# One fused attention and feed-forward block: a 2048-wide in-place VectorE exp chain, K fills by DMA, packs in one DMA, and an immediate exp bias

## The chip, the cores and the metric

The kernel runs on one core of a Trainium2 chip (trn2). The metric is the device time of one execution in microseconds (us). The median of three runs of the kernel before was 967.28 us (966.4 to 967.91). "Granted clock" is the TensorE clock that the throttle allowed, as a share of full speed.

Engine names in the profile: PE is the TensorE matmul, PEld its weight load, DVE is VectorE, ACT is ScalarE, POOL is GpSimd, SP is SyncE, which issues the DMAs.

## The reference

```python
# x [1, 2048, 512], 32 heads of 16, F = 1792, all bf16
xn = layernorm(x)
q, k, v = split(xn @ wqkv)                      # [1, 32, 2048, 16] each
p = softmax(q @ k.T * 16 ** -0.5)               # 32 x 2048 x 2048 scores
attn = (p @ v) reshaped @ wo
ffn = (silu(xn @ w1) * (xn @ w3)) @ w2          # "gate", "up", "down"
return x + attn + ffn
```

The 134 million exponentials of the softmax are the bulk of the elementwise work. In tiles of 128 x 1024 they are 1,024 tiles.

## The kernel before

The program is put in order when it is built: a small scheduler keeps a clock for each engine, with assumed durations (`dur=`), and places each instruction where it believes the engine to be free.

**Exponentials on two engines.** TensorE makes a 128 x 1024 tile of scores in PSUM. ScalarE turns most tiles into probabilities with one instruction; it has two PSUM buffers for this. VectorE takes the others through a chain of five instructions on the bits of a bf16 number (the scores come out of the matmul already scaled, so that their integer value is a bit pattern): `p1` reads PSUM, `m`, `e`, `g` split and shape the bits, `t` multiplies (in this order). The sum of `e`, `g` and `t`, made by three matmuls with V, is an approximate exponential.

```python
# ScalarE
P.op("act", lambda e: e.activation(PT[:, s_, :], ps[:, b0 * 512:(b0 + 2) * 512], ACTF.Exp,
                                   scale=ASC, bias=act_bias[:, 0:1]), ...)       # L1550
# VectorE, per tile of 1024
e.tensor_scalar(yb, ps[:, 4*512:6*512], 0.0, 32767.0, ALU.max, ALU.min)          # L1593 p1
e.tensor_scalar(dsl[.., 0], yb, 0x7F80, None, ALU.bitwise_and)                   # L1610 e
e.tensor_scalar(mb, yb, 0x7F, 0x3F00, ALU.bitwise_and, ALU.bitwise_or)           # L1616 m
e.tensor_scalar(dsl[.., 1], yb, -352.0, 0.0, ALU.add, ALU.max)                   # L1621 g
e.tensor_tensor(dsl[.., 2], yb, mb, ALU.mult)                                    # L1627 t
# ...
```

**K fills and packs.** Heads of 16 are padded to 32 partitions. The padding rows of K and Q must hold a constant, written once per group of heads (the "fills"), two groups on ScalarE and six on GpSimd. Then the real rows are moved from a staging tile by DMA (the "packs"), four DMAs of 16 partitions for each half:

```python
for g in range(2, NG):                                                           # L1157
    ... P.op("pool", lambda e: e.tensor_scalar(KT[:, g, :], sel1[:, 0:1].to_broadcast((128, S)), YB, None, ALU.mult), ...)

for j in range(4):                                                               # L1283
    m = P.dma(lambda e, j=j: e.dma_start(dst(hh)[32 * j:32 * j + 16, :],
                                         stg[64 * hh + 16 * j:64 * hh + 16 * j + 16, sl, :]), ...)
```

Of the kernel before, what the change touches and what calls it, by code (L numbers as in the profile page):

```python
# [137 lines left out]
_LAT = 0.09  # L138
# [839 lines left out]
def _plan_fast(nc, ps, flag, A_x, A_wqkv, A_wo, B_w1, B_w3, B_w2, out):  # L978
# [18 lines left out]
    ND = 3  # L997
# [4 lines left out]
    D_LAST = RPU - 6  # L1002
    NW = 3

# [6 lines left out]
    with ctx:  # L1011
        xd = sb("xd", [128, max(NT * D, ND * 3 * 1024)], I16)
        x_sb = xd[:, 0:NT * D].bitcast(BF16).rearrange("p (t d) -> p t d", d=D)
        dsl = xd[:, 0:ND * 3 * 1024].rearrange("p (s k n) -> p s k n", k=3, n=1024)
        xr = sb("xr", [128, 2, D], BF16)
        yb = sb("yb", [128, 2, 1024], I16)
        mb = sb("mb", [128, 2, 1024], I16)
# [4 lines left out]
        lnb = sb("lnb", [128, NT], FP32)  # L1022
        lnt = sb("lnt", [128, NT], FP32)
        act_bias = sb("act_bias", [128, 1], FP32)
# [8 lines left out]
        stg = sb("stg", [128, 3, 512], BF16)  # L1033
        sel = sb("sel", [128, 4], FP32)
        sel1 = sb("sel1", [128, 1], FP32)
        onorm = sb("onorm", [128, NON, 512], BF16)
# [35 lines left out]
        a_cost = lambda n: 0.113 + 0.000835 * n  # L1072
        d_cost = lambda n: 0.095 + 0.00104 * n


        def c_misc(e):
            e.memset(ones_t[:, :], 1.0)
            e.memset(mhalf[:, :], -0.5)
            e.memset(act_bias[:, :], -127.0 * math.log(2.0) + math.log(KAPPA))
            return e.memset(Vaug[:, :, :, 16:17], 1.0)  # L1080
# [5 lines left out]
        for gi in range(1, 4):  # L1086
            P.dma(lambda e, gi=gi: e.dma_start(x_sb[:, 4 * gi:4 * gi + 4, :], x_v[:, 4 * gi:4 * gi + 4, :]),
                  writes=[("x", t) for t in range(4 * gi, 4 * gi + 4)], kb=512)
            if gi == 1:
                P.dma(lambda e: e.dma_start(wv, wqkv_v[:, :, 2 * D:3 * D]), writes=[("wv",)], kb=512)  # L1090

        P.op("dve", lambda e: e.memset(bank(7), 0.0), writes=[("ps", 7)], dur=0.6)
        P.op("pool", lambda e: e.memset(sel[:, :], 1.0), writes=[("sel",)], dur=0.1)
        P.op("pool", lambda e: e.affine_select(sel[:, :], sel[:, :], [[-32, 4]], ALU.is_equal, 0.0,
                                               base=-16, channel_multiplier=1),
# [3 lines left out]
        P.op("act", lambda e: e.activation(QT[:, :, :].rearrange("p a n -> p (a n)"),  # L1099
                                           sel1[:, 0:1].to_broadcast((128, 4 * 512)), ACTF.Identity),  # L1100
             reads=[("sel1",)], writes=[("QT", i) for i in range(4)], dur=1.9)
        for g in range(2):
            P.op("act", lambda e, g=g: e.activation(KT[:, g, :], sel1[:, 0:1].to_broadcast((128, S)), ACTF.Identity,
                                                    scale=YB),
                 reads=[("sel1",)], writes=[("KT", g, i) for i in range(NQC)], dur=1.9)
        P.op("pool", c_misc, writes=[("ones_t",), ("mhalf",), ("abias",)] + [("V", t) for t in range(NT)], dur=0.8)
# [4 lines left out]
        def ln_coef(gi, n0, n1):  # L1111
            sl_ = slice(n0, n1)
            MVK = [("mv", t) for t in range(n0, n1)]

            def f(eng):
                P.op("pool", lambda e: e.tensor_scalar(lnt[:, sl_], mv[:, sl_, 1], 1.0, EPS, ALU.mult, ALU.add),
                     reads=MVK + [("mhalf",)], writes=[("lnt", n0)], dur=0.12)
                P.op("pool", lambda e: e.tensor_tensor(lnr[:, sl_], lnt[:, sl_], mhalf[:, sl_], ALU.pow),
                     reads=[("lnt", n0)], writes=[("lnr", n0)], dur=0.7)
                P.op("pool", lambda e: e.tensor_tensor(lnt[:, sl_], mv[:, sl_, 0], lnr[:, sl_], ALU.mult),  # L1120
                     reads=[("lnr", n0)] + MVK, writes=[("lnt", n0)], dur=0.12)
                o = P.op("pool", lambda e: e.tensor_scalar(lnb[:, sl_], lnt[:, sl_], -1.0, 0.0, ALU.mult, ALU.add),  # L1122
                         reads=[("lnt", n0)], writes=[("lnb", n0)], dur=0.12)
                for t in range(n0, n1):
                    P.post("dve", lambda t=t: norm(t), ready=o.end + _LAT, prio=1)
            return f
# [4 lines left out]
        def norm(t):  # L1131
            n0 = nrm0[t]
            xs = t % 4
            o = P.op("dve", lambda e: e.tensor_scalar(xn_sb[:, xs, :], x_sb[:, t, :], lnr[:, t:t + 1], lnb[:, t:t + 1],  # L1134
                                                      ALU.mult, ALU.add),
                     reads=[("x", t), ("lnr", n0), ("lnb", n0)], writes=[("xn", xs)], dur=0.25)
# [20 lines left out]
        for g in range(2, NG):  # L1157
            P.post("pool", lambda g=g: done.__setitem__(("KTi", g), P.op("pool", lambda e: e.tensor_scalar(
                KT[:, g, :], sel1[:, 0:1].to_broadcast((128, S)), YB, None, ALU.mult),
                reads=[("sel1",)], writes=[("KT", g, i) for i in range(NQC)], dur=2.5).end), ready=9.0 + g, prio=3)  # L1160
# [103 lines left out]
        def pack(dst, keys, dkeys, scale):  # L1264

            def evac(bk, o, rel):
                sl = stg_n[0] % 3
# [13 lines left out]
                def moves(hh):  # L1281
                    for j in range(4):
                        m = P.dma(lambda e, j=j: e.dma_start(dst(hh)[32 * j:32 * j + 16, :],  # L1283
                                                             stg[64 * hh + 16 * j:64 * hh + 16 * j + 16, sl, :]),
                                  reads=[("stg", sl), ("sel1",)] + keys[hh], writes=[dkeys[hh] + (j,)], kb=16)
                    done[dkeys[hh]] = m.end + _LAT
# [3 lines left out]
        def tile_KT(i, sc):  # L1290
            xc = xdone(sc * 512, 512)
            gr = []
            for c in range(DC):
# [4 lines left out]
                lambda hh: KT[:, 2 * i + hh, sc * 512:(sc + 1) * 512],  # L1298
# [3 lines left out]
        def tile_QT(qc, i):  # L1302
# [3 lines left out]
            for c in range(DC):  # L1306
# [4 lines left out]
                lambda hh: QT[:, (u0 + hh) % 4, :],  # L1311
# [122 lines left out]
        st = {"pos": 0, "pv": 0, "dpar": 0, "nd": 0, "lastA": -1.0, "n_exp": 0, "dpos": 0}  # L1434
# [3 lines left out]
        ds_free = [0.0] * ND  # L1438
# [57 lines left out]
        def score(b0, name, dur):  # L1496
# [6 lines left out]
            rd = [("QT", u % 4), ("KT", g, kt // 4)]  # L1503
            mms = []
            for i in range(2):
                j = j0 + i
                rd += [("QTm", u, j), ("KTm", g, kt // 4, j)]
# [7 lines left out]
            o = P.op("pe", f, reads=rd, writes=[("ps", b0), ("ps", b0 + 1)], dur=dur, name="%s%d" % (name, r0))  # L1515
# [7 lines left out]
        def try_a():  # L1523
# [11 lines left out]
            x = score(2 * buf, "A", 0.27)  # L1535
# [10 lines left out]
            def emit():  # L1546
# [4 lines left out]
                                                       scale=ASC, bias=act_bias[:, 0:1]),  # L1551
                         reads=[("ps", b0), ("ps", b0 + 1), ("abias",)], writes=[("PT", s_)], dur=a_cost(1024))
# [11 lines left out]

        def try_d():
# [3 lines left out]
            if r0 % RPU > D_LAST or r0 < st["dpos"]:  # L1569
                return False  # L1570
            if r0 % 4 != st["dpar"]:
                return False
            x = score(4, "D", 0.09 if st["lastA"] + 0.05 > P.t else 0.27)
# [8 lines left out]
            nd = st["nd"]  # L1582
            st["nd"] += 1
            ys = nd % 2

            def slot():
                return [s_ for s_ in range(ND) if ds_free[s_] <= P.t]

            def p1():
                s_ = slot()[0]  # L1590
                ds_free[s_] = 1e9
                left = [6]
                q = P.op("dve", lambda e: e.tensor_scalar(yb[:, ys, :], ps[:, 4 * 512:6 * 512], 0.0, 32767.0,  # L1593
                                                          ALU.max, ALU.min),
                         reads=[("ps", 4), ("ps", 5)], writes=[("yb", ys)], dur=1.24)
                dbuf[0] = q.end + _LAT

                def rel(o_):
                    left[0] -= 1
                    if left[0] == 0:  # L1600
                        ds_free[s_] = o_.end + _LAT

                def give(k, q_):
                    st["n_exp"] += (k == 2) * 2
                    for i in range(2):
                        add_task(u, j0 + i, kt, dsl[:, s_, k, 512 * i:512 * i + 512].bitcast(BF16), q_.end + _LAT,
                                 ("ds", s_, k), rel)

                def f_e():
                    q_ = P.op("dve", lambda e: e.tensor_scalar(dsl[:, s_, 0, :], yb[:, ys, :], 0x7F80, None,  # L1610
                                                               ALU.bitwise_and),
                              reads=[("yb", ys)], writes=[("ds", s_, 0)] + XD, dur=0.34)
                    give(0, q_)

                def f_m():
                    P.op("dve", lambda e: e.tensor_scalar(mb[:, ys, :], yb[:, ys, :], 0x7F, 0x3F00,  # L1616
                                                          ALU.bitwise_and, ALU.bitwise_or),
                         reads=[("yb", ys)], writes=[("mb", ys)], dur=0.34)

                def f_g():  # L1620
                    q_ = P.op("dve", lambda e: e.tensor_scalar(dsl[:, s_, 1, :], yb[:, ys, :], -352.0, 0.0,  # L1621
                                                               ALU.add, ALU.max),
                              reads=[("yb", ys)], writes=[("ds", s_, 1)] + XD, dur=0.34)
                    give(1, q_)

                def f_t():
                    q_ = P.op("dve", lambda e: e.tensor_tensor(dsl[:, s_, 2, :].bitcast(BF16),  # L1627
                                                               yb[:, ys, :].bitcast(BF16), mb[:, ys, :].bitcast(BF16),
                                                               ALU.mult),
# [289 lines left out]
```

## Time and profile before

| | before |
|---|---|
| median of the runs | 967.28 us |
| span of the profiled run | 968.4 us |
| ScalarE busy | 853.9 us, 88% |
| VectorE busy | 878.7 us, 91% |
| exponential tiles, ScalarE / VectorE | 798 / 226 |
| ScalarE idle, 0 to 80 us | 46.5 us |
| ScalarE idle, 80 to 926.5 us | 28.0 us |
| after the last exponential | 41.9 us |

These are the busy row of the page and the main groups. A group's columns are: line, engine, operation, what it writes and reads, count, then busy us in all and mean ns of one, then the engine's idle time just before the group and what ended most of it.

```profile
PE 858.6 (89%) x9033; PEld 240.4 (25%) x9033; DVE 878.7 (91%) x1437; ACT 853.9 (88%) x872; POOL 91.4 (9%) x82
...
L1550 ACT ACTIVATE f_PT<-ps,f_act_bias 128x1024 bf16<-128x1024 f32 x798 | 819.1, 1153 | 51.3 <-PE ps L1513 44.1
...
L1593 DVE TENSOR_SCALAR f_yb<-ps 128x1024 int16<-128x1024 f32 x226 | 274.4, 1214 | 5.3 <-PE ps L1513 4.9
...
L1346 ACT ACTIVATE f_th<-ps 128x512 f32<-128x512 f32 x56 | 35.2, 629 | 10.6 <-PE ps L1216 10.6
...
L1134 DVE TENSOR_SCALAR f_xn_sb<-f_xd,f_lnr,f_lnb 128x512 bf16<-128x512 bf16 x16 | 35.3, 2244 | 0.3 <-POOL f_lnb L1122 0.3
```

Read the first group twice. Its mean is 1153 ns, but 819.1 us divided by 798 is 1.026 us: consecutive exponentials overlap in the records, and the busy time counts overlapped time once. The 1.026 is what one more exponential costs a busy ScalarE.

The table by stretches of time gives each engine's busy time in each (PEclk is the granted clock):

```profile
core 0: us, PE busy (x) PEld busy (x) DVE busy (x) ACT busy (x) POOL busy (x), PEclk, DMA share, GB/s
...
20.00:40.00 20.00, 10.87 (x112) 4.12 (x104) 20.00 (x24) 5.50 (x9) 16.08 (x13) 0.70 0.44 80
...
80.00:300.00 220.00, 192.55 (x1844) 50.12 (x1844) 197.99 (x327) 199.93 (x203) 9.33 (x7) 0.94 0.23 30
300.00:600.00 300.00, 283.55 (x3009) 76.60 (x3006) 288.33 (x485) 296.20 (x301) 16.37 (x12) 0.99 0.25 29
600.00:926.50 326.50, 304.69 (x3188) 82.92 (x3186) 312.74 (x522) 322.40 (x331) 15.93 (x12) 0.99 0.25 33
926.50:968.40 41.90, 28.92 (x469) 12.55 (x469) 12.50 (x24) 1.82 (x4) 0.00 (x0) 0.86 0.20 36
```

From 80 to 926.5 us ScalarE works 818.5 of 846.5 us. From 20 to 40 us it works 5.5 of 20 us while VectorE is busy all the time. The timeline shows with what (start, duration):

```profile
25.58 0.72 DVE L1134 TENSOR_SCALAR f_xn_sb<-f_xd,f_lnr,f_lnb 128x512 bf16<-128x512 bf16 x2
26.82 10.83 DVE L1134 TENSOR_SCALAR f_xn_sb<-f_xd,f_lnr,f_lnb 128x512 bf16<-128x512 bf16 x2
...
26.77 10.73 POOL L1158 TENSOR_SCALAR f_KT<-f_sel 128x2048 bf16<-128x2048 f32 x2
```

A pair of normalising instructions takes 0.72 us alone, and the next such pair 10.83 us while GpSimd fills K. The Trainium skill, "SBUF — State Buffer", SBUF: two separate sides, describes a port pair which VectorE and GpSimd share as an exclusive lock, held for the whole instruction; this trace agrees with it.

### The profile page before, as it was taken

How to read it: one execution, taken by the hardware profiler on the slowest of the kernel's cores; microseconds unless marked ns; L12 is line 12 of the kernel's file. 1: busy time of each engine (PE TensorE's matmuls, PEld its weight loads, DVE VectorE, ACT ScalarE, POOL GpSimd, SP SyncE). 2: the span in 40 equal slices, each digit the busy share in tenths (PEclk: the TensorE clock that was granted, in tenths of full speed). 3: DMA queues.
4: the chain of work that ended last, by engine and by line, in shares of the span. 5: the costliest groups of instructions: out<-in, count | busy, mean ns of one | idle time of the engine just before them, and what ended most of it. 6: DMA issues, size and time to landing. Idle time of an engine off the chain costs nothing.

```text
span 968.4 us, 21733 instructions
## 1 busy us (share of the span) xinstructions
PE 858.6 (89%) x9033; PEld 240.4 (25%) x9033; DVE 878.7 (91%) x1437; ACT 853.9 (88%) x872; POOL 91.4 (9%) x82
## 2 busy tenths in 40 slices
PE   4669888989888999998989999999999999999985
PEld 2222122222222222222222222222222222222232
DVE  7969797999899999999999999999999999999951
ACT  3339798999899999999999999999999999999930
POOL 7840000000000000000000000000000000000000
PEclk9779799999989999999999999999999999999988
DMA  4501221312311222303232222222231212233221
GB/s 154 136 16 28 37 39 23 50 22 27 51 13 13 24 19 24 46 17 41 29 45 34 18 25 24 45 34 36 28 45 21 29 18 23 34 46 40 35 36 37
DMA packets 90685, 35.34 MB, mean 36 GB/s; under 512 B 74448, under 2 KB 88528, under 8 KB 90576
## 3 DMA queue, kind: packets, MB, share of 16 engines
q1 hardware_dynamic: 90576, 33.85, 24.7%
q8 instruction: 73, 1.20, 0.5%
q14 instruction: 36, 0.29, 0.1%
HBM read 22.81 MB, written 2.10 MB: 26 GB/s over the span
## 4 chain that ended last, share of the span: by engine, by line
ACT 43%; DVE 33%; PE 17%; issue 2%; DMA 2%; SPq 2%; DVEq 0%
ACT f_PT L1550 42%; DVE f_yb L1593 9%; PE ps L1216 8%; PE ps L1513 5%; DVE f_xd L1627 4%; PE ps L1673 4%; DVE f_xd L1610 3%; DVE f_xd L1621 3%; DVE f_mb L1616 3%; DVE f_xn_sb L1134 3%; DVE f_t L1350 2%; ACT f_th L1346 2%; SPq L1283 1%; DVE f_hT L1360 1%; DMA f_wkv<-in_A_wqkv_dram 1%
## 5 line engine op out<-in xcount | busy, mean ns | idle before, releaser
L1550 ACT ACTIVATE f_PT<-ps,f_act_bias 128x1024 bf16<-128x1024 f32 x798 | 819.1, 1153 | 51.3 <-PE ps L1513 44.1
L1513 PE MATMUL ps<-f_QT,f_KT 32*128 32x512 bf16 x2048 | 330.4, 391 | 42.4 <-ACT f_PT L1550 23.7
L1593 DVE TENSOR_SCALAR f_yb<-ps 128x1024 int16<-128x1024 f32 x226 | 274.4, 1214 | 5.3 <-PE ps L1513 4.9
L1673 PE MATMUL ps<-f_PT,f_Vaug 128*17 128x512 bf16 x1596 | 240.5, 389 | 4.5 <-DVE f_xd L1610 3.8
L1673 PE MATMUL ps<-f_xd,f_Vaug 128*17 128x512 bf16 x1356 | 238.7, 388 | 4.5 <-DVE f_xd L1610 2.9
L1216 PE MATMUL ps<-f_xnT,f_w 128*32 128x512 bf16 x1792 | 169.7, 396 | 19.4 <-DVE f_t L1350 13.8
L1513 PEld LDWEIGHTS ps<-f_QT,f_KT 32*128 32x128 bf16 x2048 | 83.0, 91 | 374.3 <-ACT f_PT L1550 291.8
L1627 DVE TENSOR_TENSOR f_xd<-f_yb,f_mb 128x1024 bf16<-128x1024 bf16 x226 | 159.5, 706 | 8.9
L1726 POOL TENSOR_TENSOR f_onorm<-f_U,f_R 128x512 bf16<-128x512 f32 x31 | 41.6, 1343 | 812.1 <-DMA f_R<-f_Rrow 532.3
L1616 DVE TENSOR_SCALAR f_mb<-f_yb 128x1024 int16<-128x1024 int16 x226 | 100.8, 446 | 5.1
L1621 DVE TENSOR_SCALAR f_xd<-f_yb 128x1024 int16<-128x1024 int16 x226 | 98.9, 438 | 7.1
L1610 DVE TENSOR_SCALAR f_xd<-f_yb 128x1024 int16<-128x1024 int16 x226 | 101.3, 448 | 0.0
L1673 PEld LDWEIGHTS ps<-f_PT,f_Vaug 128*17 128x17 bf16 x1596 | 55.4, 88 | 109.6 <-issue 83.0
L1216 PE MATMUL ps<-f_w,f_hT 128*32 128x512 bf16 x896 | 75.8, 381 | 0.5 <-DVE f_hT L1360 0.5
L1673 PEld LDWEIGHTS ps<-f_xd,f_Vaug 128*17 128x17 bf16 x1356 | 57.1, 89 | 69.6 <-issue 29.3
L1216 PEld LDWEIGHTS ps<-f_xnT,f_w 128*32 128x32 bf16 x1792 | 45.6, 96 | 70.2 <-issue 54.1
L1216 PE MATMUL ps<-f_wo,f_onorm 128*32 128x512 bf16 x512 | 46.0, 381 | 0.2 <-DVE f_wkv L1400 0.2
L1350 DVE SCALAR_TENSOR_TENSOR f_t<-f_th,ps 128x512 bf16<-128x512 f32 x56 | 38.1, 680 | 7.4 <-ACT f_th L1346 6.8
L1346 ACT ACTIVATE f_th<-ps 128x512 f32<-128x512 f32 x56 | 35.2, 629 | 10.6 <-PE ps L1216 10.6
L1360 DVE SCALAR_TENSOR_TENSOR f_hT<-f_t,ps 128x512 bf16<-128x512 bf16 x56 | 38.1, 681 | 4.1 <-PE ps L1216 2.6
L1134 DVE TENSOR_SCALAR f_xn_sb<-f_xd,f_lnr,f_lnb 128x512 bf16<-128x512 bf16 x16 | 35.3, 2244 | 0.3 <-POOL f_lnb L1122 0.3
L1216 PE MATMUL ps<-f_wkv,f_xnT 128*32 128x512 bf16 x256 | 24.4, 488 | 11.6 <-DVE f_t L1350 7.5
(54 smaller groups left out, 276.7 us busy)
## 6 DMA issues: line engine op xcount, KB each, us to landing
f_w<-in_B_w_dram SPq DMA_DIRECT2D x112, 128.0 KB, 2.8
f_R<-f_Rrow SPq DMA_DIRECT2D x128, 32.0 KB, 4.0
f_KT<-f_stg SPq DMA_DIRECT2D x128, 16.0 KB, 1.8
f_QT<-f_stg SPq DMA_DIRECT2D x128, 16.0 KB, 1.8
f_xr<-in_A_x_dram SPq DMA_DIRECT2D x16, 128.0 KB, 2.2
out_dram<-f_xn_sb SPq DMA_DIRECT2D x16, 128.0 KB, 1.9
f_w<-in_B_w_dram SPq DMA_DIRECT2D x1, 1792.0 KB
f_xd<-in_A_x_dram SPq DMA_DIRECT2D x3, 512.0 KB
```

Of the source, the lines that this page charges most:

```text
L1134: o = P.op("dve", lambda e: e.tensor_scalar(xn_sb[:, xs, :], x_sb[:, t, :], lnr[:, t:t + 1], lnb[:, t:t + 1], ALU.mult, ALU.add), reads=[( ...
L1216: ins = e.matmul(bank(bk)[32 * i:32 * i + 32, 0:ncols], make_lhsT(i), rhs_ap, start=start, stop=stop, tile_position=(0, 32 * i))
L1346: q = P.op("act", lambda e: e.activation(th[:, ss, :], bank(bk), ACTF.Tanh, scale=0.5), reads=[("ps", bk)], writes=[("th", ss)], dur=a_cos ...
L1350: q2 = P.op("dve", lambda e: e.scalar_tensor_tensor(t1[:, ss, :], th[:, ss, :], 1.0, bank(bk), ALU.add, ALU.mult), reads=[("th", ss), ("ps ...
L1513: ins = e.matmul(bank(b), l_, r_, start=True, stop=True, tile_position=(rp, 0))
L1550: q = P.op("act", lambda e: e.activation(PT[:, s_, :], ps[:, b0 * 512:(b0 + 2) * 512], ACTF.Exp, scale=ASC, bias=act_bias[:, 0:1]), reads= ...
L1593: q = P.op("dve", lambda e: e.tensor_scalar(yb[:, ys, :], ps[:, 4 * 512:6 * 512], 0.0, 32767.0, ALU.max, ALU.min), reads=[("ps", 4), ("ps" ...
L1610: q_ = P.op("dve", lambda e: e.tensor_scalar(dsl[:, s_, 0, :], yb[:, ys, :], 0x7F80, None, ALU.bitwise_and), reads=[("yb", ys)], writes=[( ...
L1616: P.op("dve", lambda e: e.tensor_scalar(mb[:, ys, :], yb[:, ys, :], 0x7F, 0x3F00, ALU.bitwise_and, ALU.bitwise_or), reads=[("yb", ys)], wr ...
L1621: q_ = P.op("dve", lambda e: e.tensor_scalar(dsl[:, s_, 1, :], yb[:, ys, :], -352.0, 0.0, ALU.add, ALU.max), reads=[("yb", ys)], writes=[( ...
L1627: q_ = P.op("dve", lambda e: e.tensor_tensor(dsl[:, s_, 2, :].bitcast(BF16), yb[:, ys, :].bitcast(BF16), mb[:, ys, :].bitcast(BF16), ALU.m ...
L1673: ins = e.matmul(bank(PV)[32 * j:32 * j + 17, :], v_, p_, start=s0, stop=s1, tile_position=(0, 32 * j))
```

## The change

The intent: less work per exponential on both engines, GpSimd out of VectorE's way at the start, and fewer DMA issues. Cut to its core (`...` marks what is left out; the two comment lines and the one after `pe_dur` stand for code that is not shown):

```diff
-    ND = 3
+    NY = 3
+    NM = 2
+    NG_ = 2
-    D_LAST = RPU - 6
+    D_PAIR = RPU - 22
+    D_LAST = RPU - 12
+    ABIAS = -127.0 * math.log(2.0) + math.log(KAPPA)
 ...
-        a_cost = lambda n: 0.113 + 0.000835 * n
-        d_cost = lambda n: 0.095 + 0.00104 * n
+        a_cost = lambda n: 0.095 + 0.000833 * n
+        d_cost = lambda n: 0.145 + 0.001045 * n
+        s_cost = lambda n: 0.18 + 0.000256 * n
 ...
-        for g in range(2, NG):
-            P.post("pool", ... P.op("pool", lambda e: e.tensor_scalar(KT[:, g, :], ...
+        def kt_fill():
+            for g in range(2, NG):
+                q = P.dma(lambda e, g=g: e.dma_start(KT[:, g, :], fsrc), ..., kb=512)
+        P.post("sp", kt_fill, ready=10.0, prio=2)
 ...
-                    for j in range(4):
-                        m = P.dma(lambda e, j=j: e.dma_start(dst(hh)[32 * j:32 * j + 16, :], ...
+                    m = P.dma(lambda e: e.dma_start(dst(hh), stg[64 * hh:64 * hh + 64, sl, :]), ..., kb=64)
 ...
-                lambda hh: KT[:, 2 * i + hh, sc * 512:(sc + 1) * 512],
+                lambda hh: KT[0:128:2, 2 * i + hh, sc * 512:(sc + 1) * 512],
 ...
-                                                       scale=ASC, bias=act_bias[:, 0:1]),
+                                                       scale=ASC, bias=ABIAS),
 ...
+            # two score tiles share one slot: p1 twice (1024 each, from PSUM), then m, g, t, e
+            # on 2048 columns; t and e overwrite their inputs in place
+                sl = dcur[0] = {..., "max": 2 if rr <= D_PAIR else 1}
 ...
+        def pe_dur(mode, rows=None):     # new assumed TensorE durations for the scheduler
```

The layernorm steps on GpSimd became fewer too, and ScalarE's fills write the same bits as float32 with half the columns (two of 1.89 us before). The new assumed durations change the order of all engines' instructions. The split of exponentials is now 810 tiles on ScalarE and 214 on VectorE (95 pairs and 24 singles).

## The prediction

> **What bounds the kernel now.** Span 968.4 us; the engine table has ScalarE busy 853.9 us (88%), VectorE 878.7 (91%), TensorE 858.6 (89%, padded by matmul latency). Exponentials are shared out at schedule time: 798 tiles of 128x1024 on ScalarE, 226 on VectorE. The chain of waits is 42% ScalarE exp. The table by stretches shows three parts: 0-80 us, where ScalarE idles 46 us; 80-925 us, where it is busy 817 of 845 us and is the limit; a tail of some 42 us on TensorE and DMA. From 20 to 60 us VectorE is always busy, with normalising ops (16, mean 2244 ns); the timeline has a pair at 0.72 us when GpSimd does not fill K and at 10.8 us when it does. So VectorE and GpSimd block each other there (K fills 32.2 us, normalising 35.3).
>
> **Costs of the change.**
> 1. Immediate exp bias. Back to back an exp takes 1.026 us (819.1/798); alone 1.11. Without a bias operand a 512-wide ScalarE op takes 0.60 and a 2048-wide one 1.89, so a 1024-wide one takes 1.03 alone: 0.08 less, some 0.94 back to back (estimate). The Trainium skill, "ScalarE: Activation LUTs", What ACT_TABLE_LOAD costs, gives about 93 ns per pointer operand, near this. The new program has 810 exps: 761 us instead of 819. With tanh (35), transposes' evictions (8) and fills (4 of 1 us) ScalarE comes to 808 us, all on the critical path.
> 2. VectorE chain 2048 wide. Now 1214+446+448+438+706 = 3252 ns per tile. At 2048 the skill's "VectorE: DVE Perf Modes", perf-mode tier table, has 693 ns for one-source ops and 1224 for products (no such width in this trace); a pair then costs about 2.43+2.1+1.24 = 5.77 instead of 6.50 us. The new order has 214 VectorE tiles (95 pairs, 24 singles): 627 us instead of 735. VectorE falls to about 740 us and is no longer near the limit.
> 3. K fills by DMA, fewer GpSimd steps. Normalising falls to about 0.35 us each, 30 us off VectorE in the first 60. The fills put 3 MB into a busy early queue ahead of the first K and Q packs; packs become 64 DMAs instead of 256 (the first eight held the queue 5 us). I expect 15-20 us less ScalarE idle.
> 4. Tail: 188 gate/up matmuls follow the last score instead of 96: 6 us more.
> 5. TensorE work hardly changes (8985 matmuls for 9033), but must fit in less time: ScalarE stalls stay near 28 us or grow to 40.
>
> **Sum.** ScalarE 808 - 4 (tanh in the tail) + early idle 28 + stalls 28 + tail 48 = 908 us. Eight times in ten: 886 to 932. Chances: faster by over 2% 0.95, within 2% 0.04, slower 0.01.
>
> **What would show each step.** Exp back to back at 0.93-0.95 us, ScalarE over 95% busy from 100 to 850 us; wide ops near 0.70 and 1.24 us, VectorE busy about 80%; normalising below 0.5 us and the early part ending near 50-55 us; a tail of 46-50 us.
>
> **What would make it wrong.** TensorE, in order, may not refill ScalarE's two buffers within 0.94 us, and ScalarE would idle 60 us or more (930-945). The fills may hold up the first packs and gate/up weights, and eat the early gain. If the early part closes by 45 us and stalls fall below 20, 890.

## More of the kernel before

**Row sums.** The softmax denominators come out of the PV matmul (the probabilities times V) as an extra row. After each of 32 units VectorE copies the result out of PSUM (`U`), a small DMA moves the sums (`f_Lc<-f_U`), and VectorE takes the reciprocal (L1708). The weights of gate and up go through a ring of three buffers (`NW = 3`), one block of 2 x 128 KB for each pair of feed-forward tiles.

Most of the 28 us in the middle are between 80 and 300 us. A part of them was not understood when the prediction was written; it is this, VectorE's timeline and that of the SyncE queue:

```profile
151.72 0.68 DVE L1690 COPY f_U<-ps 128x512 f32<-128x512 f32 x1
...
159.00 0.25 DVE L1708 RECIPROCAL f_Rc<-f_Lc 128x16 f32<-128x16 f32 x1 [3.98 <-DMA f_Lc<-f_U]
...
148.82 8.17 SPq L1283 DMA_DIRECT2D f_KT<-f_stg  x13
157.09 0.61 SPq L1696 DMA_DIRECT2D f_Lc<-f_U  x1
```

The `U` copy ends at 152.40. The small DMA of the row sums is ready to go, but the queue is issuing pack DMAs, 0.63 us each, and gets to it at 157.09: some seven of them were still in front. (The view starts at 149 us and shows 13 packs; from 138 us it shows 16 in a row.) VectorE, in order, stands still for 3.98 us at the reciprocal. There are five such waits in the run, 13.7 us in all.

## The result, and the profile after

| | before | after |
|---|---|---|
| median of the runs | 967.6 us (966.4 to 973.5, 4 runs) | 886.0 us (883.9 to 888.35, 4 runs) |
| ratio | | 0.9135, 95% interval [0.9102, 0.9169] |
| span of the profiled run | 968.4 us | 886.3 us |
| ScalarE busy | 853.9 us | 791.6 us |
| VectorE busy | 878.7 us (91%) | 766.3 us (86%) |
| ScalarE idle, early part | 46.5 us (to 80) | 27.1 us (to 54, and still to 80) |
| ScalarE idle, middle | 28.0 us (to 926.5) | 11.3 us (to 826.4) |
| after the last exponential | 41.9 us | 59.9 us |

A ratio compares the fast runs of one kernel with those of the other in the same rounds, so it is not quite the ratio of the medians quoted. The change is 8.65% faster. The outputs are right. The direction was right; the time is 22 us below the predicted 908 and sits on the lower edge of the range, or just under it (0.9135 of 967.6 is 883.9 us).

The busy row and the groups after, as shown of before:

```profile
PE 797.7 (90%) x8985; PEld 223.4 (25%) x8985; DVE 766.3 (86%) x999; ACT 791.6 (89%) x885; POOL 59.4 (7%) x59
...
L1571 ACT ACTIVATE f_PT<-ps 128x1024 bf16<-128x1024 f32 x810 | 761.3, 1094 | 21.4 <-PE ps L1533 18.1
...
L1623 DVE TENSOR_SCALAR f_xd<-ps 128x1024 int16<-128x1024 f32 x214 | 261.2, 1221 | 33.9 <-PE ps L1533 26.4
...
L1350 ACT ACTIVATE f_th<-ps 128x512 f32<-128x512 f32 x56 | 38.0, 679 | 26.9 <-PE ps L1222 26.9
```

An exponential now costs 761.3/810 = 0.940 us, 0.086 less. The ScalarE groups add up to 812.5 us and the engine row says 791.6: an overlap of 20.9 us between groups. The timeline shows where it comes from, a tanh of the feed-forward part between exponentials:

```profile
541.45 3.77 ACT L1571 ACTIVATE f_PT<-ps 128x1024 bf16<-128x1024 f32 x4
545.06 0.64 ACT L1350 ACTIVATE f_th<-ps 128x512 f32<-128x512 f32 x1
545.54 2.00 ACT L1571 ACTIVATE f_PT<-ps 128x1024 bf16<-128x1024 f32 x2
```

The tanh is 0.64 us long in its record, but the next exponential starts 0.48 us after it, and the tanh itself starts 0.16 us before the exponential in front of it ends. So a tanh costs ScalarE less than its duration.

The table by stretches, after:

```profile
core 0: us, PE busy (x) PEld busy (x) DVE busy (x) ACT busy (x) POOL busy (x), PEclk, DMA share, GB/s
...
20.00:40.00 20.00, 16.61 (x216) 6.67 (x212) 18.79 (x43) 10.77 (x15) 6.36 (x11) 0.91 0.87 207
...
80.00:300.00 220.00, 206.67 (x2142) 52.31 (x2134) 195.70 (x247) 213.28 (x235) 11.62 (x9) 0.91 0.24 31
300.00:600.00 300.00, 279.77 (x3156) 75.31 (x3152) 277.18 (x344) 297.48 (x333) 20.98 (x13) 1.00 0.27 33
600.00:826.40 226.40, 209.67 (x2368) 57.21 (x2364) 213.90 (x273) 224.31 (x250) 12.26 (x9) 1.00 0.26 33
826.40:886.30 59.90, 38.47 (x563) 15.76 (x563) 16.13 (x29) 3.61 (x7) 0.00 (x0) 0.79 0.19 38
```

From 80 to 300 us ScalarE is idle for 6.7 us, where it was 20.1. The normalising instructions and the wide operations of the chain, one line for each shape:

```profile
L1138 DVE TENSOR_SCALAR f_xn_sb<-f_xd,f_mv,f_lnr 128x512 bf16<-128x512 bf16 x16 | 8.5, 567 | 0.6 <-POOL f_lnr L1126 0.6
...
L1669 DVE TENSOR_TENSOR f_xd<-f_xd 128x2048 bf16<-128x2048 bf16 x95 | 116.0, 1221 | 0.0
L1683 DVE TENSOR_SCALAR f_xd<-f_xd 128x2048 int16<-128x2048 int16 x95 | 71.9, 756 | 1.5
L1662 DVE TENSOR_SCALAR f_xd<-f_xd 128x2048 int16<-128x2048 int16 x95 | 68.7, 723 | 6.0 <-PE ps L1736 3.7
```

The normalising fell from 2244 to 567 ns. The wide ones shown take 723 and 756 ns (int16) and 1221 (the product) on average. The Trainium skill, "VectorE: DVE Perf Modes", The perf-mode tier table, has 693 and 1224 ns for 2048 columns of bf16, and this trace agrees with both. The means of the one-source operations are lifted by a few long ones: from 60 to 820 us the 253 that run beside no GpSimd operation take 688 to 691 ns by line, none over 696, and the 27 that overlap one (GpSimd scales the attention output there) take up to 1753. One of those starts at 307.32 us, while such an operation runs from 307.10 to 308.38, and ends at 308.92. This looks like the block of the start again, for some 12 us of VectorE's time in the middle (an estimate from these means); no run here takes it away.

In the tail TensorE has new waits, for gate and up weights:

```profile
829.72 1.32 PE L1222 MATMUL ps<-f_xnT,f_w 128*32 128x512 bf16 x12 [2.32 <-DMA f_w<-in_B_w_dram]
...
835.82 2.74 PE L1222 MATMUL ps<-f_xnT,f_w 128*32 128x512 bf16 x32 [2.83 <-DMA f_w<-in_B_w_dram]
842.20 3.60 PE L1222 MATMUL ps<-f_xnT,f_w 128*32 128x512 bf16 x32 [3.64 <-DMA f_w<-in_B_w_dram]
848.41 3.18 PE L1222 MATMUL ps<-f_xnT,f_w 128*32 128x512 bf16 x28 [2.61 <-DMA f_w<-in_B_w_dram]
```

That is 11.4 us in four waits; in the tail of before there was one of 2.8 us. With 208 gate and up matmuls left after the last score, the ring of three buffers empties faster than its loads land. (The prediction's 188 and 96 count only the unbroken run at the end; in the traces 208 follow the last score after the change and 112 before, so the difference is nearly the same.)

**The account.** The span is ScalarE's busy time, plus its idle time in the early part, in the middle and in the tail (the tail less the ScalarE work in it: 59.9 - 3.6).

| term | predicted | measured | difference |
|---|---|---|---|
| ScalarE work | 808 | 791.6 | -16.4 |
| early idle | 28 | 27.1 | -0.9 |
| stalls in the middle | 28 | 11.3 | -16.7 |
| tail, less ScalarE work in it | 44 (48 - 4) | 56.3 | +12.3 |
| sum | 908 | 886.3 | -21.7 |

### The profile page after: what moved, and what is told of

Its sections match the earlier page's. It is cut to its first block, busy times and chain, and to the rows that moved or that the text cites. A ratio compares the mean times of both kernels' runs of the same rounds, so it can differ in the third digit from the quotient of the medians.

```text
span 886.3 us, 21031 instructions
## 1 busy us (share of the span) xinstructions
PE 797.7 (90%) x8985; PEld 223.4 (25%) x8985; DVE 766.3 (86%) x999; ACT 791.6 (89%) x885; POOL 59.4 (7%) x59
## 4 chain that ended last, share of the span: by engine, by line
ACT 60%; PE 20%; DVE 15%; DMA 2%; issue 2%; SPq 0%; DVEq 0%
ACT f_PT L1571 57%; PE ps L1222 10%; PE ps L1533 6%; DVE f_xd L1623 5%; PE ps L1736 4%; DVE f_xd L1669 3%; ACT f_th L1350 2%; DVE f_xd L1683 2%; DVE f_xd L1662 1%; DVE f_xd L1678 1%; DMA f_w<-in_B_w_dram 1%; DMA f_wkv<-in_A_wqkv_dram 1%; DVE f_hT L1364 1%; DVE f_t L1354 1%; DVE f_xn_sb L1412 1%
## 5 line engine op out<-in xcount | busy, mean ns | idle before, releaser
L1571 ACT ACTIVATE f_PT<-ps 128x1024 bf16<-128x1024 f32 x810 | 761.3, 1094 | 21.4 <-PE ps L1533 18.1
L1533 PE MATMUL ps<-f_QT,f_KT 32*128 32x512 bf16 x2048 | 330.2, 395 | 38.7 <-ACT f_PT L1571 30.1
L1623 DVE TENSOR_SCALAR f_xd<-ps 128x1024 int16<-128x1024 f32 x214 | 261.2, 1221 | 33.9 <-PE ps L1533 26.4
L1736 PE MATMUL ps<-f_PT,f_Vaug 128*17 128x512 bf16 x1620 | 232.3, 394 | 5.1 <-DVE f_xd L1678 1.6
L1736 PE MATMUL ps<-f_xd,f_Vaug 128*17 128x512 bf16 x1284 | 182.0, 393 | 3.0 <-DVE f_xd L1683 0.9
L1222 PE MATMUL ps<-f_xnT,f_w 128*32 128x512 bf16 x1792 | 157.2, 401 | 18.2 <-DMA f_w<-in_B_w_dram 11.4
L1669 DVE TENSOR_TENSOR f_xd<-f_xd 128x2048 bf16<-128x2048 bf16 (+1 forms) x119 | 132.4, 1112 | 0.0
L1662 DVE TENSOR_SCALAR f_xd<-f_xd 128x2048 int16<-128x2048 int16 (+1 forms) x119 | 78.8, 662 | 6.3 <-PE ps L1736 4.1
L1683 DVE TENSOR_SCALAR f_xd<-f_xd 128x2048 int16<-128x2048 int16 (+1 forms) x119 | 82.0, 689 | 2.0
L1678 DVE TENSOR_SCALAR f_xd<-f_xd 128x2048 int16<-128x2048 int16 (+1 forms) x119 | 78.3, 658 | 2.6
L1350 ACT ACTIVATE f_th<-ps 128x512 f32<-128x512 f32 x56 | 38.0, 679 | 26.9 <-PE ps L1222 26.9
L1736 PEld LDWEIGHTS ps<-f_xd,f_Vaug 128*17 128x17 bf16 x1284 | 41.1, 88 | 43.9 <-issue 22.3
L1222 PE MATMUL ps<-f_wo,f_onorm 128*32 128x512 bf16 x512 | 40.2, 381 | 0.2 <-DVE f_wkv L1404 0.2
L1222 PEld LDWEIGHTS ps<-f_w,f_hT 128*32 128x32 bf16 x896 | 20.8, 96 | 23.0 <-issue 9.5
L1222 PE MATMUL ps<-f_wkv,f_xnT 128*32 128x512 bf16 x256 | 21.3, 434 | 3.5 <-DMA f_wkv<-in_A_wqkv_dram 3.5
```

What stands on the lines that cost most here:

```text
L1222: ins = e.matmul(bank(bk)[32 * i:32 * i + 32, 0:ncols], make_lhsT(i), rhs_ap, start=start, stop=stop, tile_position=(0, 32 * i))
L1350: q = P.op("act", lambda e: e.activation(th[:, ss, :], bank(bk), ACTF.Tanh, scale=0.5), reads=[("ps", bk)], writes=[("th", ss)], dur=a_cos ...
L1533: ins = e.matmul(bank(b), l_, r_, start=True, stop=True, tile_position=(rp, 0))
L1571: q = P.op("act", lambda e: e.activation(PT[:, s_, :], ps[:, b0 * 512:(b0 + 2) * 512], ACTF.Exp, scale=ASC, bias=ABIAS), reads=[("ps", b0) ...
L1623: q = P.op("dve", lambda e: e.tensor_scalar(dsl[:, ys, 1024 * c:1024 * c + 1024], ps[:, 4 * 512:6 * 512], 0.0, 32767.0, ALU.max, ALU.min), ...
L1662: P.op("dve", lambda e: e.tensor_scalar(dsl[:, NY + m_, 0:n], y, 0x7F, 0x3F00, ALU.bitwise_and, ALU.bitwise_or), reads=[("ds", ys)], write ...
```

## The experiments

Twelve kernels ran (there is no run e8 in the record), all with correct results. Differences between an experiment and the changed kernel are given in points of the time of before, from the ratios to before of each one's own rounds (one point is about 9.7 us). First, parts of the change undone in the changed kernel.

**Exp bias from a tile again** (same order of instructions):

```diff
-   scale=ASC, bias=ABIAS)
+   scale=ASC, bias=act_bias[:, 0:1])
```

> The kernel after, with one part undone: the exp bias is again read from a [128,1] tile; the order on every engine is the same. Theory A (ScalarE is the limit in the middle part, so its whole saving counts): exp back to back goes from 0.940 to about 1.026 us, 810 x 0.086 = 70 us more, 950 to 960 us, ScalarE busy about 860 us, VectorE busy unchanged near 766. Rival (TensorE cannot refill two buffers in 0.94 us, so part of the saving had turned into stalls): less than 40 us more, below 925, with ScalarE idle in the middle part falling clearly below 11 us.

Measured: 948.78 us, ratio 0.9767 [0.9725, 0.9809]. So 6.3 points of the gain are lost by this part alone. The exponentials take 833.5/810 = 1.029 us again and ScalarE is busy 858.4 us instead of 791.6. Theory A holds, with a time slightly under 950 us. The 0.089 us per exponential agree with the 93 ns that the Trainium skill, "ScalarE: Activation LUTs", What ACT_TABLE_LOAD costs, gives for a per-partition pointer operand.

**K fills on GpSimd again:** the `kt_fill` block is replaced by the loop of before.

> The kernel after, with one part undone: K groups 2 to 7 are filled by GpSimd again (six ops), not by DMA. The plan changes slightly (811 exps on ScalarE, 184 gate/up matmuls in the tail for 188). Theory A (port lock): normalising ops return to about 2 us on average, ScalarE idle in the early part from 27 to about 45 us, 15 to 20 us more, 901-906. Rival (the early gain comes from the packs and the shorter GpSimd chain): under 6 us more.

Measured: 901.85 us, ratio 0.9284; 1.5 points. The normalising is back at 1899 ns, and in the first 54 us ScalarE is busy 18.5 us instead of 26.9. Theory A holds in time, but ScalarE's idle time to 80 us rises only to 38.7 us and not to 45; it is also idle more in the middle.

**Packs as four DMAs again:**

```diff
-   m = P.dma(lambda e: e.dma_start(dst(hh), stg[64 * hh:64 * hh + 64, sl, :]), ...)
+   for j in range(4):
+       m = P.dma(lambda e, j=j: e.dma_start(dst(hh, j), stg[64 * hh + 16 * j:64 * hh + 16 * j + 16, sl, :]), ...)
```

> The kernel after, with one part undone: each pack is four DMAs of 16 partitions again (256 instead of 64). Same number of tiles on each engine; 208 gate/up matmuls in the tail for 188, worth 1 to 2 us. Theory P (the middle stalls of before came from the packs: VectorE's reciprocal, in order, waited 11.7 us in 80-300 us for the row-sum DMA that stood in the queue behind eight packs of 0.6 us each): VectorE waits for that DMA return, ScalarE idle in the middle part from 11 to 20 us or more, 9 to 16 us more in all, 895-902. Rival (the new order, which counts TensorE's mode switches, removed the stalls): within 4 us of the kernel after.

Measured: 917.78 us, ratio 0.9468 [0.9416, 0.952]; 3.3 points, at least twice what was expected. VectorE's waits from 60 to 830 us show the reciprocal again (us in all, times, longest):

```profile
DVE f_Rc L1773 <- DMA f_Lc<-f_U: 8.8, 3, 3.1
```

After the change there is only one such wait, of 2.0 us, in the tail. ScalarE's waits for score tiles rose to 30.2 us in that window, from 8.1 after the change in a window that ends 10 us earlier. From 60 us to its last exponential ScalarE is idle for 34.1 us, where it was 11.3 after the change. So the single DMA is worth more than the issue time at the start: it takes away middle stalls. The reciprocal's waits are only 8.8 us of this; how the rest comes about was not taken apart. A rival for a part of it: the granted clock was 0.938 to 0.950 in these runs and 0.961 to 0.969 after the change.

**The chain alone:** the changed kernel with pointer bias, four packs and GpSimd fills, all three of the edits above.

> The wide in-place chain with its plan alone: the kernel after with pointer bias, four DMAs per pack and GpSimd fills all back (811 exps, 184 gate/up matmuls in the tail). If the costs of undoing each part of the kernel after simply added up (62, 32 and 16 us), it would take 996 us. Theory A (in before both engines are full, and this part relieves only VectorE, while it hands 13 tiles to ScalarE and lengthens the tail): no gain, 965 to 996. Rival (VectorE was the limit of before): 950 or less.

Measured: 975.81 us, ratio 1.0071 [1.0037, 1.0105]. The wide chain and the new order bring nothing by themselves (the shorter GpSimd layernorm and the cheaper ScalarE fills are still in this kernel): VectorE's busy time falls to 790.2 us, but ScalarE still has 860.4 us to do. Theory A.

Then parts of the change done alone in the kernel of before.

**Immediate bias alone** (the order is unchanged):

> The kernel before, with one part done alone: the immediate exp bias; the order is that of before. Theory A (the parts need each other): VectorE was busy 799 of 847 us in the middle part of before, so it becomes the limit; the time falls only 20 to 35 us, to 933-948, and ScalarE idles 40 us or more in the middle part, waiting for scores. Rival (ScalarE alone was the limit): 798 x 0.086 = 68 us less, about 900.

Measured: 962.49 us, ratio 0.9934 [0.9882, 0.9986]. The same edit that is worth 6.3 points in the changed kernel is worth 0.7 here. Expectation A had the direction and not the size. The stretch from 80 to 880 us, where ScalarE was busy 772.3 us in the kernel before, and its waits from 60 to 880 us:

```profile
80.00:880.00 800.00, 738.59 (x7684) 199.90 (x7682) 760.32 (x1269) 738.23 (x794) 40.09 (x30) 0.98 0.25 31
...
ACT f_PT L1550 <- PE ps L1513: 46.9, 58, 9.1
ACT f_PT L1550 <- PE ps L1673: 18.2, 47, 1.4
```

The middle of ScalarE's time is 34 us less busy and 34 us more idle. In the kernel before these two waits were 34.6 and 5.7 us in the same window. TensorE, which works in order, waited less for ScalarE there (9.2 us for 21.3 before) and no less for VectorE: 21.2 us for the feed-forward product (20.7 before), 11.7 for `p1` (8.5) and 9.6 for `e` (6.5). VectorE was busy 95% of the stretch from 80 to 880 us, after 94% before. So both engines limited the kernel before, and speeding up one alone turned into waiting for the other.

**One pack DMA alone** (the row pattern is made stride-2 too):

> The kernel before, with one part done alone: packs as one stride-2 DMA each. Theory P (the issue queue with its 0.6 us per DMA made VectorE wait 11.7 us for row sums): those waits go, ScalarE idle in the middle part from 28 to 12-16 us, and the early part gains a little from faster packs: 10 to 18 us less, 952-960. Rival (VectorE is so full in before that the stalls come back elsewhere): under 5 us less.

Measured: 948.92 us, ratio 0.9786 [0.9758, 0.9814]; 2.1 points. The waits of the reciprocal between 80 and 820 us (11.7 us in four before) are gone, and ScalarE's idle time from 60 us to its last exponential falls from 35.9 to 15.9 us. That is the whole gain: theory P, with a little more than expected.

**Fill DMA alone:**

> The kernel before, with one part done alone: K groups 2 to 7 filled by DMA from one tile that ScalarE fills. Theory (port lock in the early part): normalising ops fall to 0.6 us or less, ScalarE idle before 75 us from 46 to 30 us, 10 to 18 us less, 952-960; the packs, still four DMAs each, now stand behind 3 MB of fills, which may eat some of it. Rival (nothing gained because the packs stand in the queue): under 5 us less.

Measured: 936.0 us, ratio 0.9661 [0.9623, 0.9698]; 3.4 points, about twice the upper end of the expectation. The normalising falls to 617 ns. ScalarE's idle time before 80 us falls from 46.5 to 25.8 us, where the theory had 30; the other 13 us come later (9 us less idle time in the middle and a tail shorter by 7, against some 3 us more of ScalarE work). The planned split and order moved too (799 and 225 tiles), so those are not shown to be the fill's own.

| part | alone on before | undone from after |
|---|---|---|
| immediate bias | -0.7 | 6.3 |
| one pack DMA | -2.1 | 3.3 |
| fill DMA | -3.4 | 1.5 |
| chain and order | +0.7 | see the next group |

Alone they add up to -5.5 points, together they bring -8.65. Each entry is uncertain by some 0.3 to 0.6 points.

The third group asks about the chain's width, the order and the tail.

**Narrow chain:** everything of the change, but no pairs.

```diff
-    D_PAIR = RPU - 22
+    D_PAIR = -1
```

> The kernel after, with the VectorE chain 1024 wide for all tiles (still in place and interleaved). The plan then gives VectorE 191 tiles for 214 and ScalarE 833 exps for 810, and leaves 8 gate/up matmuls for the tail instead of 188. Theory A (the width is worth what it moves off ScalarE): 23 x 0.94 = 22 us more on ScalarE, about 15 us less tail, 5 to 10 us more in all, 890-897. Rival (VectorE itself is the limit in the kernel after): 20 us or more, above 906, with ScalarE idle in the middle part over 20 us.

Measured: 869.92 us (867.92 to 870.74), ratio 0.8964 [0.8943, 0.8985], so 1.7 points **faster** than the change. Both theories fell. The scheduler plans the narrow chain as slower and so gives VectorE only 191 tiles and ScalarE 833. ScalarE's waits from 60 to 820 us, first after the change, then in the narrow run:

```profile
ACT f_PT L1571 <- PE ps L1533: 8.1, 21, 0.9
ACT f_PT L1571 <- PE ps L1736: 2.0, 7, 0.3
```

```profile
ACT f_PT L1571 <- PE ps L1533: 1.9, 5, 0.6
ACT f_PT L1571 <- PE ps L1736: 0.3, 1, 0.3
...
54.00:837.30 783.30, 726.09 (x8020) 192.11 (x8016) 675.18 (x1165) 780.22 (x872) 40.59 (x31) 0.99 0.26 34
837.30:866.20 28.90, 19.98 (x357) 9.46 (x357) 7.83 (x17) 0.00 (x0) 0.00 (x0) 0.92 0.23 38
```

ScalarE is idle 3.1 us in 783, and with only 8 gate and up matmuls left the tail is 28.9 us.

Why does the width gain so little? Start to start, and not by durations: from 300 to 800 us I took each chain operation after which the next VectorE operation began within 0.15 us of its end, and averaged the time from start to start.

| us per tile | m | e | g | t | p1 | sum |
|---|---|---|---|---|---|---|
| before, 1024 | 0.373 | 0.463 | 0.477 | 0.638 | 1.217 | 3.17 |
| narrow chain, 1024 | 0.376 | 0.353 | 0.501 | 0.637 | 1.147 | 3.01 |
| after (1.76 tiles per chain) | 0.649 | 0.664 | 0.704 | 1.099 | 1.177 | (3.116 / 1.76) + 1.177 = 2.95 |

VectorE operations overlap by up to 0.09 us when the next one waits for nothing: narrow one-source operations of 0.42 us start 0.34 us apart (medians). The reordered narrow chain is 5% below before per tile, the width takes another 2% in this mix, and 4% if the full pairs are taken alone (2.90 us). The prediction, with 627 us for 214 tiles against 3.25 us per tile, had 10%, and the traces show 7%. Its 2.93 us for the new tile is right; the 3.25 of the old one, a sum of durations, was too high. The 0.42 us of a narrow operation are mostly not a fixed cost that a wider one saves.

**Wide chain, the narrow run's split:** at most six VectorE tiles per unit (190 against 834).

```diff
-            if rr > D_LAST or r0 % 4 != st["dpar"]:
+            if rr > D_LAST or r0 % 4 != st["dpar"] or nd_unit[r0 // RPU] >= 6:
```

> The kernel after with the wide chain, but at most six VectorE tiles per unit: 190 tiles in 95 pairs and 834 exps, the split of the narrow run (191 and 833), and 20 gate/up matmuls in the tail. Theory S (the narrow run was faster because of its split: the middle ends with the gate/up work done, so the tail is short; the width itself is neutral): 866 to 876. Rival W (wide ops cost by themselves, their 1.2 us hold up evictions): 880 or more, with ScalarE idle in the middle part above 12 us.

Measured: 882.84 us, ratio 0.9102 [0.9077, 0.9127]; 0.3 points faster than the change (the intervals overlap, so these two are even), 1.4 slower than the narrow chain with nearly the same split. So the split is not the reason; the wide chain costs some 13 us with it, 9 of them as idle time of ScalarE in the middle. That is rival W in time; its mechanism does not show, since TensorE's waits for the eviction `U` are 3.3 us from 60 to 820 us and 0.6 in the narrow run. ScalarE is idle some 12 us in the middle, 6.3 of them from 200 to 300 us, where the granted clock was 0.80. In the narrow run that stretch has a clock of 0.93 and 2.4 us idle. The mean clock of the whole run is 0.983 to 0.989 in the narrow runs and 0.960 to 0.964 here. The other profiles lean the same way: from 200 to 300 us the clock is 0.80 to 0.83 in six of the eight kernels with a wide chain (0.86 and 0.94 in the other two) and 0.91 to 0.98 in all six with a narrow one. Whether the bursts of a wide chain lower the clock, or the clock is low for another reason and stalls ScalarE, these runs do not tell.

**Old assumed durations:** the changed kernel, put in order with before's `a_cost`, `d_cost` and TensorE durations.

> The kernel after, planned with the durations that the scheduler of before assumed for ScalarE, copies and TensorE (no mode switches). The instructions are the same, their order is not; the plan has 805 exps for 810 and leaves 36 gate/up matmuls in the tail for 188. Theory A (the order matters little to ScalarE's stalls, which came from the packs): ScalarE idle in the middle part stays below 20 us and the shorter tail shows: 872-884. Rival (the better durations keep ScalarE fed): idle in the middle part rises to 25 us or more and the time to 890-905.

Measured: 888.96 us, ratio 0.9173 [0.9138, 0.9207]; 0.4 points slower, with overlapping intervals, so even. The time lies between the two ranges, but ScalarE's idle time from 60 us to its last exponential is 29.5 us, as the rival said. The parts moved: ScalarE's waits for tiles in the middle rose from 10.1 us (60 to 820 us) to 23.1 (60 to 830), and the tail became shorter, 31.7 us for 59.9. The better durations keep ScalarE fed, and pay for it with work left over for the tail (36 gate and up matmuls here, 208 after the change).

**Weights of the tail early:** the changed kernel with its last six gate and up weight blocks loaded into K groups that are no longer needed.

```diff
+        NTL = 6
+        def wslot(idx):            # the last six blocks live in K groups 0 to 2
+            ...
+        for i_ in range(NTL):
+            P.post("sp", lambda i_=i_: load_w13(T0 + i_), ready=200.0, prio=4,
+                   cond=lambda i_=i_: st["pos"] >= (NU - NG + i_ // 2 + 2) * RPU)
```

> The kernel after, with the last six gate/up weight blocks loaded ahead into K groups 0 to 2, which nobody reads after unit 26 of 32, instead of the three rotating slots. Theory (in the tail TensorE waits four times, 11.4 us in all, for weight loads that can only start when a slot is free): those waits go, 8 to 12 us less, 874-878; the plan leaves 208 gate/up matmuls for the tail for 188, worth 1 us. Rival (the tail is bound by something else, such as the last unit's row-sum chain of DMAs, which lands at 841 us): under 4 us less.

Measured: 871.05 us (869.74 to 875.26, 5 runs), ratio 0.8979 [0.8954, 0.9005]; 1.6 points faster than the change. TensorE's waits in the tail, first after the change (826 to 886 us), then here (820 to 875 us):

```profile
PE ps L1222 <- DMA f_w<-in_B_w_dram: 11.4, 4, 3.6
```

```profile
PE ps L1235 <- DVE f_t L1367: 2.7, 1, 2.7
PE ps L1235 <- ACT f_PT L1584: 1.1, 1, 1.1
```

The last exponential ends at 827.35 of 872.4 us: the tail is 45.0 us instead of 59.9, with the same number of gate and up matmuls in the trace (208; the expectation's "208 for 188" compares two ways of counting). The weight loads explain the tail's whole excess over the predicted 48.

**Both together:** narrow chain, durations near its spacing and `D_LAST = RPU - 8` (809 and 215 tiles), weights early.

> The two things that beat the changed kernel, put together: the chain 1024 wide, planned with VectorE durations near its start-to-start times (so 809 wide exponentials on ScalarE and 215 tiles on VectorE, against 833 and 191 in the narrow run), and the last six gate and up weight blocks loaded early. Theory: ScalarE stays nearly gapless, has 24 exponentials of 0.94 us (22.6 us) less than the narrow run, but more feed-forward work is left for the tail, now free of waits for weights: 855 to 866 us, last exponential near 818 to 826, middle idle under 10 us. Rival: VectorE with 24 tiles more (about 67 us at 2.8 us) has too little slack (it was busy 766 us of 886 with 214 tiles in the changed kernel), so it is late, ScalarE stalls again by 10 us or more in the middle, and the time is no better than the 870 of the narrow run.

Measured: 877.06 us (873.38 to 881.38, 6 runs), ratio 0.9027 [0.9, 0.9055]. The rival was right. VectorE is busy 793.2 of 879.2 us, and ScalarE's waits from 60 to 820 us are larger than in either of the kernels it was made of:

```profile
ACT f_PT L1584 <- PE ps L1546: 19.3, 33, 1.4
```

24 tiles more on VectorE leave it little slack: from 60 us to the last exponential it is busy 94% of the time, and 86% in the narrow run. The best versions stay the narrow chain (869.92) and the early weights (871.05). Early weights with the narrow run's split of 833 and 191 were not tried.

## Why the prediction was right or wrong

- **Right: direction, the bias and the start.** The bias was costed at 0.94 us per exponential and measured 0.940; removing it again cost 6.3 of the 8.65 points. The early idle was predicted as 28 us and was 27.1. The port lock between GpSimd and VectorE was read rightly; undoing the fill showed it.
- **Wrong: "With tanh (35), transposes' evictions (8) and fills (4 of 1 us) ScalarE comes to 808 us, all on the critical path."** This term was mis-sized by 16.4 us. It adds up groups whose durations overlap at their borders. The engine row measured 791.6. The hint was in the profile of before: its groups add up to 869.0, its row to 853.9.
- **Wrong: "ScalarE stalls stay near 28 us or grow to 40."** They were 11.3. The prediction took all stalls of the middle for a TensorE that cannot refill ScalarE's buffers. Part of them came from the queue of 16 KB packs in front of the row-sum DMA. One pack DMA in the kernel before took 20 us of ScalarE's idle time from the middle, four packs in the changed kernel brought 23 us back, each time with the reciprocal's waits vanishing or appearing. The old assumed durations also brought stalls back, 13 us of waits. Which part of the 16.7 us belongs to the packs and which to the order is not separated, since the parts do not add.
- **Wrong: "188 gate/up matmuls follow the last score instead of 96: 6 us more."** The tail grew by 18 us, from 41.9 to 59.9. The prediction counted TensorE's time for the extra matmuls (96 by the traces, 92 by its count) and not that the ring of three weight buffers would be read faster than it is filled: 11.4 us of waits. With these loads made early, the tail was 45.0 us.
- **Wrong, at little cost here: the width's gain.** "VectorE falls to about 740 us and is no longer near the limit": it was 766.3 us, 86% and not 80%. The sum was made of durations, not of spacings: it took 108 us off for the chain (735 to 627), but by the traces the chain occupies 704.3 us of VectorE before and 614.8 after, 90 us less; the rest fell by 24 us and not by 30. The narrow run shows that the width was not needed at all, and the chain alone that this part gains nothing by itself.
- **Small misses:** the normalising took 0.567 us and not below 0.5; the early part ended near 54 us, within the predicted 50 to 55.

Two terms were some 16 us too high each and one 12 us too low. That the time came so near the range is in part luck: the tail's error hid about a third of the other two. Sized rightly, the first alone would have put the forecast at 892 us.

## What to carry to other kernels

Build a prediction from engine rows and from spacings, start to start, of the instructions, not from sums of group durations; check it first by making the same sum for the kernel before. When two engines are both about 90% busy, one part done alone says little about its worth: the immediate bias was worth 0.7 points before and 6.3 after the others. Where a change ends the bound stage earlier, look at what its tail then needs (here weights from a small ring), and look for small DMAs that wait in a queue behind many others.

## What the Trainium skill lacked or had wrong

- "DMA: Bandwidth & Descriptors", Anatomy of one DMA, lists some 50 ns of sequencer dispatch for the GpSimd path. For how long one DMA holds the SyncE queue of this chip I found no time on the page; its only such figure, 512 sequencer cycles for "previous generations", stands in a section on another chip. Here a pack DMA held the queue for 0.63 us and the row-sum DMA for 0.61, so the packs still in front of a ready row-sum DMA held it back by 4.7 us.
- Nothing that the runs show contradicts the passages named above: 693 and 1224 ns for the wide operations (688 to 691 and 1221 here) and 93 ns for a pointer operand (89 here).
